# Moving the identity's blocks and the query spreads of a decode attention kernel from VectorE to GpSimd, and taking row sums as repeated matmul weights

## The chip, the cores and the metric

One core of one Trainium2 chip. The metric is the device time of one execution in microseconds (us). Before the change it was 1344.0 us, the median of 3 runs (1343.92 to 1344.07).

## The reference, cut to what matters

```python
B, Sq, D = 4, 1, 1024
H, Sk, Dh = 32, 8192, 128
q = reshape(x @ wq)                              # B, H, 1, Dh
scores = einsum("bhqd,bhkd->bhqk", q, k_cache) * Dh ** -0.5
o = einsum("bhqk,bhkd->bhqd", softmax(scores), v_cache)
a = reshape(o) @ wo
# B: a gated MLP on one token per batch, F = 3584 (w_gate, w_up, w_down)
return g * a + (1 - g) * b                       # g = sigmoid((x * gate_w).sum(-1))
```

All tensors are bf16. The key and the value cache hold 4 x 32 x 8192 x 128 elements each, 268 MB apiece. Every byte is read once and used for one query row, so this is a kernel that streams.

## The kernel before

The caches are read as 32 key blocks and 32 value blocks of 4 heads (8.39 MB, two halves of 4.19 MB). They go through a ring of five slots in SBUF, each half a block in size. A load is issued by SyncE as soon as the slot's last reader has finished.

```python
NS = 5
ring = const.tile([P, NS, RING], BF, name="ring")      # 5 slots of 32 KB per partition
def load_pair(src, n, apart=False):                     # two slots, one or two DMAs
    a = slots(2)
    if a + 1 < NS and not apart:
        nc.sync.dma_start(out=flat[:, lo:lo + 2 * n], in_=src)      # [cut]
    ...                                                 # else one DMA for each half
```

A key block is turned piece by piece on VectorE (eight 128x2048 transposes) and multiplied on TensorE with the four queries. The weights of these matmuls are a window into a tile `Z` that is zero except for the query values. Writing those values into `Z` is the "spread". It is done for the next block while a block is being worked on; there are two `Z` tiles.

```python
def spread(d):
    b, h0 = heads(d)
    Z = Zt[d % 2]
    nc.vector.tensor_tensor(out=Z[:, :, QP - 1:QP - 1 + P].rearrange("p e (q c) -> p e q c", c=QP)[:, :, :, 0],
                            in0=qa[:, :, h0:h0 + NQ, b], in1=mq[:].to_broadcast([P, 4, NQ]), op=ALU.mult)

def k_pair(d):
    ...                                                 # [cut] Z, sps
    ks = load_pair(kv_view(A_k_cache, d), RING)
    for n in range(RD):                                 # 8 pieces
        kn, c = ks[n // JT], n % JT
        nc.vector.transpose(out=flat_t.bitcast(U32),
                            in_=kn[:, c * CJ * Dh:(c + 1) * CJ * Dh].bitcast(U32))
        ...                                             # [cut] 8 matmuls with windows of Z
        if n == JT // 2 and d + 1 < ND:
            spread(d + 1)                               # JT // 2 == 2: after the third piece
    if t == GD - 1:
        softmax(g)                                      # after each group of four blocks
```

Four key blocks make a group. `softmax` leaves the row sums `rs` [128 x 1]. A total for each head is then a matmul of the row sums, spread by a mask, with a matrix of ones:

```python
rex = stat.tile([P, GH], F32, tag="rex")
nc.vector.tensor_scalar(out=rex[:], in0=mask, scalar1=rs[:, 0:1], scalar2=None, op0=ALU.mult)
def inverse():
    nc.tensor.matmul(tot[:, :], lhsT=ones[:], rhs=rex[:], start=True, stop=True)
    ...
```

GpSimd has, before the change, only some memsets and half of the copies that bring a group's probabilities from `PT` to `PB` (ScalarE does the other half). Value block d - 4 follows key block d on TensorE. The engines' order of work is fixed by the program: an engine does its instructions in the order in which they are written.

Of the kernel before, what the change touches and what calls it, by code (L numbers as in the profile page):

```python
# [8 lines left out]
BF = mybir.dt.bfloat16  # L9
F32 = mybir.dt.float32  # L10
U32 = mybir.dt.uint32
ACT = mybir.ActivationFunctionType
ALU = mybir.AluOpType
AX = mybir.AxisListType
# [98 lines left out]
def kernel(  # L113
# [15 lines left out]
    nc = tc.nc  # L129
    P = 128  # L130
# [4 lines left out]
    NQ = 4  # L135
    QP = P // NQ
# [5 lines left out]
    GH = GD * NQ  # L142
# [14 lines left out]
    const = ctx.enter_context(tc.tile_pool(name="const", bufs=1))  # L157
    ptp = ctx.enter_context(tc.tile_pool(name="ptp", bufs=1))
    stat = ctx.enter_context(tc.tile_pool(name="stat", bufs=2))
# [39 lines left out]
    def small(shape, dtype=F32):  # L199
        return mps.tile(shape, dtype, name="small", tag="small")  # L200
# [15 lines left out]
        nc.vector.memset(z[:], 0.0)  # L216
    acc = acc4[0:Bn].rearrange("p z n -> p (z n)")

    row = const.tile([P, P], F32)
    nc.vector.memset(row[:, 0:1], 0.0)  # L220
    n = 1
    while n < P:
        nc.vector.tensor_scalar(out=row[:, n:2 * n], in0=row[:, 0:n], scalar1=float(n), scalar2=None, op0=ALU.add)
        n *= 2
    col = const.tile([P, 32], F32)
    nc.vector.transpose(out=col[:].bitcast(U32), in_=row[:, 0:32].bitcast(U32))
    for n in range(32, P, 32):
        nc.vector.tensor_scalar(out=col[n:n + 32], in0=col[n:n + 32], scalar1=float(n), scalar2=None, op0=ALU.add)
    ident = const.tile([P, P], F32)
    nc.vector.tensor_scalar(out=ident[:], in0=row[:], scalar1=col[:, 0:1], scalar2=None, op0=ALU.is_equal)  # L230
    identb = const.tile([P, P], BF)
    nc.vector.tensor_copy(out=identb[:], in_=ident[:])
    xw_ps = small([P, DT, NX], BF)
# [5 lines left out]
    R = ptp.tile([P, 4, P], BF, name="R", tag="PTs")  # L239
    for half in range(2):  # L240
        for e in range(2):
            turns = ident[:, 64 * half + e:64 * half + 64:2]
            for n in range(4):
                nc.vector.tensor_copy(out=R[:, 2 * half + e, 32 * n:32 * n + 32], in_=turns)

    mask3 = const.tile([P, GD, NQ], F32)
    nc.vector.tensor_reduce(out=mask3[:], in_=ident[:].rearrange("p (q t r) -> p t q r", q=NQ, t=GD), axis=AX.X, op=ALU.add)
    mask = mask3[:].rearrange("p t q -> p (t q)")
    selg = const.tile([P, 4, GD, NQ], F32)
    one = ident[:].rearrange("p (t e s a) -> p e a t s", t=GD, e=2, s=NQ)  # L250
    for a in range(4):
        nc.vector.tensor_tensor(out=selg[:, a], in0=one[:, 0, a], in1=one[:, 1, a], op=ALU.add)
    mE4 = const.tile([P, 2, 4], F32)
    nc.vector.tensor_reduce(out=mE4[:], in_=ident[:].rearrange("p (n e r) -> p e n r", n=4, e=2), axis=AX.X, op=ALU.add)
    mE = const.tile([P, 2], F32)
    nc.vector.tensor_reduce(out=mE[:], in_=mE4[:], axis=AX.X, op=ALU.add)
    mq4 = const.tile([P, NQ], F32)
    nc.vector.tensor_reduce(out=mq4[:], in_=ident[:].rearrange("p (q r) -> p q r", q=NQ), axis=AX.X, op=ALU.add)
    mq = const.tile([P, 1, NQ], BF)
    nc.vector.tensor_copy(out=mq[:, 0, :], in_=mq4[:])  # L260
    ones = const.tile([P, P], F32)
    nc.gpsimd.memset(ones[:], 1.0)
    mx, mxT, ng, ngT = [const.tile([P, 32], F32, name=f"mx{i}") for i in range(4)]
    nc.vector.memset(mx[:], 0.0)
    ZW = QP - 1 + P + 1
    Zt = [const.tile([P, 4, ZW], BF, name=f"Z{i}") for i in range(2)]
    PB = const.tile([P, QP, 2, 2, 2, NQ, 4], BF, name="PB")
# [5 lines left out]
    qa = const.tile([P, 4, H, Bn], BF)  # L273
# [143 lines left out]
    def heads(d):  # L417
        return divmod(d * NQ, H)
# [5 lines left out]
    def spread(d):  # L424
        b, h0 = heads(d)
        Z = Zt[d % 2]
        nc.vector.tensor_tensor(out=Z[:, :, QP - 1:QP - 1 + P].rearrange("p e (q c) -> p e q c", c=QP)[:, :, :, 0],  # L427
                                in0=qa[:, :, h0:h0 + NQ, b], in1=mq[:].to_broadcast([P, 4, NQ]), op=ALU.mult)

    def k_pair(d):  # L430
        g, t = divmod(d, GD)
        Z = Zt[d % 2]
        if d == 0:
            spread(0)
        if t == 0:
            S_ps[g] = scp.tile([P, 2, 512], F32, name="S_ps")
        sps = S_ps[g]
        ks = load_pair(kv_view(A_k_cache, d), RING)
        for n in range(RD):
            kn, c = ks[n // JT], n % JT  # L440
            flat_t = turned(P, CJ * P)
            T = flat_t.rearrange("p (j h i e) -> p j h i e", j=CJ, h=2, e=2)
            nc.vector.transpose(out=flat_t.bitcast(U32),  # L443
                                in_=kn[:, c * CJ * Dh:(c + 1) * CJ * Dh].bitcast(U32))
            s = QP - 1 - (RD * t + n)
            for he in range(4):
                half, e = divmod(he, 2)
                for z in range(2):
                    nc.tensor.matmul(sps[:, z, :], lhsT=Z[:, he, s:s + P], rhs=T[:, 16 * z:16 * z + 16, half, :, e],  # L449
                                     start=(t == 0 and n == 0 and he == 0),  # L450
                                     stop=(t == GD - 1 and n == RD - 1 and he == 3))
            if n == JT // 2 and d + 1 < ND:
                spread(d + 1)
            if n == JT:
                flush()
            if n == JT + 2:
                flush_late()
        if t == GD - 1:
            softmax(g)

    def softmax(g):
        sps = S_ps.pop(g)

        nc.vector.tensor_reduce(out=mx[:, 0:1], in_=sps[:].rearrange("p z n -> p (z n)"), axis=AX.X, op=ALU.max)  # L464
        nc.vector.transpose(out=mxT[:].bitcast(U32), in_=mx[:].bitcast(U32))
        gm = stat.tile([P, GD], F32, tag="gm")
        nc.vector.tensor_reduce(out=gm[:], in_=mxT[:].rearrange("p (t r) -> p t r", r=RD), axis=AX.X, op=ALU.max)
        nc.vector.tensor_scalar(out=ng[:].rearrange("p (t r) -> p t r", r=RD), in0=gm[:].unsqueeze(2).to_broadcast([P, GD, RD]),
                                scalar1=-scale, scalar2=None, op0=ALU.mult)
        nc.vector.transpose(out=ngT[:].bitcast(U32), in_=ng[:].bitcast(U32))  # L470
        negm = ngT
        PTs = ptp.tile([P, 1024], BF, name="PTs", tag="PTs")
        rs = stat.tile([P, 1], F32, tag="rs")
        nc.scalar.activation(out=PTs[:], in_=sps[:].rearrange("p z n -> p (z n)"), func=ACT.Exp, bias=negm[:, 0:1], scale=scale, accum_out=rs[:, 0:1])  # L474
        PT = ptp.tile([P, 32, 32], BF, name="PT")
        nc.vector.transpose(out=PT[:].rearrange("p j i -> p (j i)"), in_=PTs[:])  # L476
        rex = stat.tile([P, GH], F32, tag="rex")
        nc.vector.tensor_scalar(out=rex[:], in0=mask, scalar1=rs[:, 0:1], scalar2=None, op0=ALU.mult)

        def inverse():  # L480
            tot = small([P, GH])
            nc.tensor.matmul(tot[:, :], lhsT=ones[:], rhs=rex[:], start=True, stop=True)  # L482
            rinv = stat.tile([P, GH], F32, name="rinv", tag="rinv")
            nc.vector.reciprocal(out=rinv[:], in_=tot[:, :])  # L484
            rinv_t[g] = rinv
        late.append(inverse)

        def spread_p():
            Pv = PT[:].rearrange("p (q j) i -> p i q j", j=4)
            Bv = PB[:].rearrange("p i z w e s j -> p i (z w e) s j")  # L490
            for q in range(NQ):
                at = slice(QP * q, QP * (q + 1))
                if q % 2 == 0:
                    nc.scalar.copy(out=Bv[at, :, :, q, :], in_=Pv[at])  # L494
                else:
                    nc.gpsimd.tensor_copy(out=Bv[at, :, :, q, :], in_=Pv[at])  # L496
        behind.append(spread_p)
# [125 lines left out]
```

## Time and profile before

| | before |
|---|---|
| time, median | 1344.0 us |
| bytes moved, span of the profiled run | 576.18 MB, 1342.0 us |
| DMA share and rate, 0 to 1321 us | 1.00, 432 GB/s |
| busy: TensorE, VectorE, GpSimd | 77%, 46%, 3% |
| VectorE's waits for key DMAs | 485.6 us |

The page of the profile of before. PE is TensorE, PEld its weight loads, DVE VectorE, ACT ScalarE, POOL GpSimd. The rows of digits cut the span into 40 slices; a digit is the busy share in tenths, 9 for 90% or more. The last two lines are the chain of waits, by engine and by line: the work that ended last, followed back.

```profile
span 1342.0 us, 7617 instructions
...
PE 1037.2 (77%) x4552; PEld 228.1 (17%) x2364; DVE 621.8 (46%) x434; ACT 50.6 (4%) x46; POOL 35.5 (3%) x24
...
DVE  3555655545346554336455556046555254556000
...
DMA  9999999999999999999999999999999999999997
GB/s 416 437 432 430 436 436 427 447 428 421 441 426 429 443 436 423 437 434 430 438 434 430 432 427 436 436 432 438 428 425 433 432 433 440 436 419 446 419 424 327
...
DMA 69%; DVE 19%; PE 11%; issue 0%; ACT 0%; SPq 0%; DVEq 0%
DMA ring<-in_A_k_cache_dram 58%; DVE TB L443 19%; DMA ring<-in_A_v_cache_dram 7%; PE o_ps L523 7%; PE S_ps L449 3%; DMA ring<-in_B_w_gate_dram 3%; DMA ring<-in_A_wo_dram 1%; PE o_ps L315 0%; DVE Z L427 0%; PE acc L315 0%; PE acc L281 0%; PE small L482 0%; PE small L543 0%; DVE OS L536 0%; ACT OS L535 0%
```

The reader is to see the DMA row, full to the last slice, beside a VectorE row of fives. The chain of waits gives VectorE 19%, but this is not a limit by itself: a DMA that is issued when a buffer comes free appears in the chain behind whatever freed the buffer, even if other transfers keep the DMA engines busy meanwhile. The table of stages (a stretch of the span, its length, the busy time of each engine with its instructions, granted TensorE clock, DMA share, GB/s) settles it:

```profile
core 0: us, PE busy (x) PEld busy (x) DVE busy (x) ACT busy (x) POOL busy (x), PEclk, DMA share, GB/s
...
0.00:1321.00 1321.00, 1021.15 (x4464) 224.20 (x2309) 619.92 (x430) 49.35 (x44) 35.48 (x24) 0.90 1.00 432
1321.00:1337.50 16.50, 14.31 (x81) 3.66 (x52) 1.23 (x3) 0.69 (x1) 0.00 (x0) 1.00 0.84 343
```

Until 1321 us the DMA engines are busy all the time: the share is 1.00. The Trainium skill, "SBUF — State Buffer", section "SBUF: two separate sides", names about 436 GB/s as the peak of the DMA side of SBUF; the 432 GB/s of this trace agree.

The issues of DMAs on the same page (KB each, and median us from issue to landing) show that half a key block, 4096 KB, takes 34.2 us, of which its own bytes need about 9.7 us at 432 GB/s; it stands behind other transfers for the rest. (The 14 halves are those of the 7 key blocks that go over the end of the ring and so take two DMAs.)

```profile
ring<-in_A_k_cache_dram SPq DMA_DIRECT2D x14, 4096.0 KB, 34.2
```

What the change touches on VectorE, from the groups of instructions by form (line, engine, operation, output<-inputs, shapes, count | busy us, mean ns | idle us just before, and what ended it), and the only large group on GpSimd:

```profile
L443 DVE STREAM_TRANSPOSE TB<-ring 128x2048 uint32<-128x2048 uint32 x256 | 569.4, 2280 | 487.7 <-DMA ring<-in_A_k_cache_dram 485.6 <-PE S_ps L449 2.1
...
L427 DVE TENSOR_TENSOR Z<-qa,mq 128x16 bf16<-128x16 bf16 x32 | 6.0, 189 | 0.0
...
L478 DVE TENSOR_SCALAR rex<-mask,rs 128x16 f32<-128x16 f32 x8 | 1.5, 193 | 0.0
```

```profile
L496 POOL COPY PB<-PT 32x1024 bf16<-32x1024 bf16 x16 | 30.5, 1905 | 1223.9 <-PE o_ps L523 1069.8 <-DVE rex L478 153.6
```

One steady period of the chain of waits (start, length, what):

```profile
364.96 6.70 DVE TB L443 x3
371.66 0.11 DVE Z L427
371.77 10.95 DVE TB L443 x5
382.72 0.04 issue
382.76 1.90 PE S_ps L449 x8
384.66 13.93 PE o_ps L523 x64
398.61 34.40 DMA ring<-in_A_k_cache_dram
```

The stream needs 16.78 MB / 432 GB/s = 38.8 us for the pair.

### The profile page before, as it was taken

To read this page: it belongs to the slowest core of one execution; us is meant where nothing else is said; L and a number is where in the kernel's file an instruction comes from. 1 tells how busy PE (TensorE), PEld (TensorE's weight loads), DVE (VectorE), ACT (ScalarE), POOL (GpSimd) and SP (SyncE) were. 2 spreads that over 40 slices of the span, in tenths; PEclk is the share of its full clock that TensorE was granted. 3 is DMA by queue.
4 is the path that set the end of the run, shared out by engine and by line. 5 is a ranking of instruction groups with operands and counts; after the bars stand their busy time and mean duration, and the time that the engine had idled before them with its cause. 6 is when DMAs were issued, how large, how long until landed. Compare 5 with 4: busy or idle time off the path is not lost.

```text
span 1342.0 us, 7617 instructions
## 1 busy us (share of the span) xinstructions
PE 1037.2 (77%) x4552; PEld 228.1 (17%) x2364; DVE 621.8 (46%) x434; ACT 50.6 (4%) x46; POOL 35.5 (3%) x24
## 2 busy tenths in 40 slices
PE   2565878787788687778987779597778678877898
PEld 0111111111111121111211112111111112111222
DVE  3555655545346554336455556046555254556000
ACT  0000100001000010001000010000100010000100
POOL 1000100001000010001000010000100010000100
PEclk9777988988998888899988889898889799888999
DMA  9999999999999999999999999999999999999997
GB/s 416 437 432 430 436 436 427 447 428 421 441 426 429 443 436 423 437 434 430 438 434 430 432 427 436 436 432 438 428 425 433 432 433 440 436 419 446 419 424 327
DMA packets 14316, 576.18 MB, mean 429 GB/s; under 512 B 1598, under 2 KB 1606, under 8 KB 2252
## 3 DMA queue, kind: packets, MB, share of 16 engines
q1 hardware_dynamic: 14276, 575.69, 99.5%
q8 instruction: 27, 0.44, 0.1%
q14 instruction: 5, 0.04, 0.0%
q10 hardware_dynamic: 8, 0.00, 0.0%
HBM read 575.68 MB, written 0.01 MB: 429 GB/s over the span
## 4 chain that ended last, share of the span: by engine, by line
DMA 69%; DVE 19%; PE 11%; issue 0%; ACT 0%; SPq 0%; DVEq 0%
DMA ring<-in_A_k_cache_dram 58%; DVE TB L443 19%; DMA ring<-in_A_v_cache_dram 7%; PE o_ps L523 7%; PE S_ps L449 3%; DMA ring<-in_B_w_gate_dram 3%; DMA ring<-in_A_wo_dram 1%; PE o_ps L315 0%; DVE Z L427 0%; PE acc L315 0%; PE acc L281 0%; PE small L482 0%; PE small L543 0%; DVE OS L536 0%; ACT OS L535 0%
## 5 line engine op out<-in xcount | busy, mean ns | idle before, releaser
L443 DVE STREAM_TRANSPOSE TB<-ring 128x2048 uint32<-128x2048 uint32 x256 | 569.4, 2280 | 487.7 <-DMA ring<-in_A_k_cache_dram 485.6
L449 PE MATMUL S_ps<-TB,Z 128*128 128x512 bf16 x2048 | 522.8, 411 | 216.5 <-DVE TB L443 216.0
L523 PE MATMUL o_ps<-ring,PB 128*32 128x512 bf16 x2048 | 461.3, 387 | 52.5 <-DMA ring<-in_A_v_cache_dram 48.0
L449 PEld LDWEIGHTS <-Z 128*128 128x128 bf16 x1024 | 106.1, 104 | 628.4 <-issue 626.8
L523 PEld LDWEIGHTS <-PB 128*32 128x32 bf16 x1024 | 100.5, 98 | 404.9 <-issue 394.9
L496 POOL COPY PB<-PT 32x1024 bf16<-32x1024 bf16 x16 | 30.5, 1905 | 1223.9 <-PE o_ps L523 1069.8
L474 ACT ACTIVATE PTs<-S_ps,mx 128x1024 bf16<-128x1024 f32 x8 | 8.9, 1114 | 1019.7 <-DVE mx L470 1019.7
L536 DVE SCALAR_TENSOR_TENSOR OS<-o_ps,mE,OS 128x512 f32<-128x512 f32 x8 | 6.0, 751 | 70.8 <-ACT OS L535 70.8
L494 ACT COPY PB<-PT 32x1024 bf16<-32x1024 bf16 x16 | 30.6, 1910 | 1.6 <-DVE PT L476 1.4
L484 DVE RECIPROCAL rinv<-small 128x16 f32<-128x16 f32 x8 | 2.1, 258 | 41.5 <-PE small L482 41.5
L378 DVE CAST LT<-small 128x64 bf16<-128x64 f32 x2 | 0.5, 225 | 44.0 <-PE small L376 44.0
L235 PE MATMUL small<-identb,x 6*128 6x6 bf16 x8 | 0.6, 197 | 22.2 <-DMA x<-in_A_x_dram 22.2
L464 DVE TENSOR_REDUCE mx<-S_ps 128x1 f32<-128x1024 f32 x8 | 9.8, 1225 | 15.9 <-PE S_ps L449 15.9
L281 PE MATMUL acc<-ring,LT 128*4 128x512 bf16 x64 | 14.8, 379 | 1.7 <-DMA ring<-in_A_wo_dram 0.9
L476 DVE STREAM_TRANSPOSE PT<-PTs 128x1024 bf16<-128x1024 bf16 x8 | 10.0, 1245 | 10.2 <-ACT PTs L474 10.2
L281 PE MATMUL acc<-ring,hT 128*4 128x512 bf16 x56 | 12.2, 379 | 0.0
L535 ACT ACTIVATE OS<-o_ps,mE 128x512 f32<-128x512 f32 x8 | 5.5, 687 | 163.4 <-PE o_ps L523 163.4
L543 PEld LDWEIGHTS small<-selg,OS 128*128 128x128 f32 x64 | 8.4, 195 | 4.1 <-issue 3.9
L315 PE MATMUL o_ps<-ring,xw 128*4 128x512 bf16 x56 | 5.3, 505 | 3.9 <-DMA ring<-in_B_w_gate_dram 3.9
L543 PE MATMUL small<-selg,OS 128*128 128x16 f32 x64 | 8.1, 259 | 0.0
L237 DVE COPY xw<-small 128x48 bf16<-128x48 bf16 x1 | 0.2, 182 | 14.9 <-PE small L235 14.9
L315 PE MATMUL S_ps<-ring,xw 128*4 128x512 bf16 x64 | 6.3, 582 | 0.3 <-DVE xw L237 0.3
(68 smaller groups left out, 72.6 us busy)
## 6 DMA issues: line engine op xcount, KB each, us to landing
ring<-in_A_k_cache_dram SPq DMA_DIRECT2D x14, 4096.0 KB, 34.2
ring<-in_A_v_cache_dram SPq DMA_DIRECT2D x14, 4096.0 KB, 31.3
ring<-in_B_w_gate_dram SPq DMA_DIRECT2D x1, 7168.0 KB, 37.2
ring<-in_B_w_up_dram SPq DMA_DIRECT2D x1, 7168.0 KB, 39.2
ring<-in_B_w_down_dram SPq DMA_DIRECT2D x2, 3584.0 KB, 27.3
ring<-in_A_wo_dram SPq DMA_DIRECT2D x6, 1024.0 KB, 24.7
ring<-in_A_v_cache_dram SPq DMA_DIRECT2D x2, 2048.0 KB, 30.5
ring<-in_A_v_cache_dram SPq DMA_DIRECT2D x4, 1024.0 KB, 24.6
```

The source lines that it names most:

```text
L281: nc.tensor.matmul(out_ap, lhsT=lhsT, rhs=rhs, start=start, stop=True, skip_group_check=True)
L315: nc.tensor.matmul(ps[32 * k:32 * k + Bn, z, :], lhsT=xT[TW * half + t], rhs=cols(w, t, 4 * z + k), start=(half + t == 0), stop=(half == 1 ...
L443: nc.vector.transpose(out=flat_t.bitcast(U32), in_=kn[:, c * CJ * Dh:(c + 1) * CJ * Dh].bitcast(U32))
L449: nc.tensor.matmul(sps[:, z, :], lhsT=Z[:, he, s:s + P], rhs=T[:, 16 * z:16 * z + 16, half, :, e], start=(t == 0 and n == 0 and he == 0), ...
L464: nc.vector.tensor_reduce(out=mx[:, 0:1], in_=sps[:].rearrange("p z n -> p (z n)"), axis=AX.X, op=ALU.max)
L474: nc.scalar.activation(out=PTs[:], in_=sps[:].rearrange("p z n -> p (z n)"), func=ACT.Exp, bias=negm[:, 0:1], scale=scale, accum_out=rs[:, ...
L476: nc.vector.transpose(out=PT[:].rearrange("p j i -> p (j i)"), in_=PTs[:])
L494: nc.scalar.copy(out=Bv[at, :, :, q, :], in_=Pv[at])
L496: nc.gpsimd.tensor_copy(out=Bv[at, :, :, q, :], in_=Pv[at])
L523: nc.tensor.matmul(o_ps[row:row + NM, e, :], lhsT=PB[:, RD * t + c, z, w].rearrange("p e s j -> p (e s j)"), rhs=vn[:, j0 * Dh:(j0 + 4) * ...
L536: nc.vector.scalar_tensor_tensor(out=o_sb[:], in0=o_ps[:, 1, :], scalar=mE[:, 1:2], in1=o_sb[:], op0=ALU.mult, op1=ALU.add)
L543: nc.tensor.matmul(oT[:, :], lhsT=o_sb[:, q * Dh:(q + 1) * Dh], rhs=selg[:, q].rearrange("p t s -> p (t s)"), start=(q == 0), stop=(q == 3))
```

## The change

The intent was to relieve VectorE: the query spread becomes four copies on GpSimd, one for each quarter of the partitions, so no mask is needed. The identity is made of four copies of a 32x32 identity, also on GpSimd, as are the casts into `R` (16 on VectorE before, 4 larger ones now). The product of row sums and mask goes away, because the row sums become the matmul's weights, repeated over 128 columns, and the mask itself its operand.

```diff
+    nc.vector.tensor_tensor(out=id32[:], in0=row[:, 0], in1=row[:, 1], op=ALU.is_equal)
     ident = const.tile([P, P], F32)
-    nc.vector.tensor_scalar(out=ident[:], in0=row[:], scalar1=col[:, 0:1], scalar2=None, op0=ALU.is_equal)
+    nc.gpsimd.memset(ident[:], 0.0)
+    for n in range(0, P, 32):
+        nc.gpsimd.tensor_copy(out=ident[n:n + 32, n:n + 32], in_=id32[n:n + 32])
 [cut: rows and columns are counted to 32 only; masks mE4, mq4, mq and the ones are gone]
-            turns = ident[:, 64 * half + e:64 * half + 64:2]
-            for n in range(4):
-                nc.vector.tensor_copy(out=R[:, 2 * half + e, 32 * n:32 * n + 32], in_=turns)
+            nc.gpsimd.tensor_copy(out=R[:, 2 * half + e].rearrange("p (n j) -> p n j", n=4),
+                                  in_=ident[:, 64 * half + e:64 * half + 64:2].unsqueeze(1).to_broadcast([P, 4, 32]))
 [cut]
-        nc.vector.tensor_tensor(out=Z[:, :, QP - 1:QP - 1 + P].rearrange("p e (q c) -> p e q c", c=QP)[:, :, :, 0],
-                                in0=qa[:, :, h0:h0 + NQ, b], in1=mq[:].to_broadcast([P, 4, NQ]), op=ALU.mult)
+        for q in range(NQ):
+            at = slice(QP * q, QP * (q + 1))
+            nc.gpsimd.tensor_copy(out=Z[at, :, QP - 1 + QP * q], in_=qa[at, :, h0 + q, b])
 [cut]
-        rex = stat.tile([P, GH], F32, tag="rex")
-        nc.vector.tensor_scalar(out=rex[:], in0=mask, scalar1=rs[:, 0:1], scalar2=None, op0=ALU.mult)
-            nc.tensor.matmul(tot[:, :], lhsT=ones[:], rhs=rex[:], start=True, stop=True)
+            nc.tensor.matmul(tot[:, :], lhsT=rs[:, 0:1].to_broadcast([P, P]), rhs=mask, start=True, stop=True)
```

More of the change, by code (lines that the diff above doesn't have):

```diff
@@ L217 @@
     acc = acc4[0:Bn].rearrange("p z n -> p (z n)")
-    row = const.tile([P, P], F32)
-    nc.vector.memset(row[:, 0:1], 0.0)
+    row = const.tile([P, 2, 32], F32)
+    nc.vector.memset(row[:, 0, 0:1], 0.0)
     n = 1
-    while n < P:
-        nc.vector.tensor_scalar(out=row[:, n:2 * n], in0=row[:, 0:n], scalar1=float(n), scalar2=None, op0=ALU.add)
+    while n < 32:
+        nc.vector.tensor_scalar(out=row[:, 0, n:2 * n], in0=row[:, 0, 0:n], scalar1=float(n), scalar2=None, op0=ALU.add)
         n *= 2
-    col = const.tile([P, 32], F32)
-    nc.vector.transpose(out=col[:].bitcast(U32), in_=row[:, 0:32].bitcast(U32))
-    for n in range(32, P, 32):
-        nc.vector.tensor_scalar(out=col[n:n + 32], in0=col[n:n + 32], scalar1=float(n), scalar2=None, op0=ALU.add)
+    nc.vector.transpose(out=row[:, 1].bitcast(U32), in_=row[:, 0].bitcast(U32))
+    id32 = const.tile([P, 32], F32)
+    nc.vector.tensor_tensor(out=id32[:], in0=row[:, 0], in1=row[:, 1], op=ALU.is_equal)
     ident = const.tile([P, P], F32)
-    nc.vector.tensor_scalar(out=ident[:], in0=row[:], scalar1=col[:, 0:1], scalar2=None, op0=ALU.is_equal)
+    nc.gpsimd.memset(ident[:], 0.0)
+    for n in range(0, P, 32):
+        nc.gpsimd.tensor_copy(out=ident[n:n + 32, n:n + 32], in_=id32[n:n + 32])
     identb = const.tile([P, P], BF)
@@ L252 @@
         nc.vector.tensor_tensor(out=selg[:, a], in0=one[:, 0, a], in1=one[:, 1, a], op=ALU.add)
-    mE4 = const.tile([P, 2, 4], F32)
-    nc.vector.tensor_reduce(out=mE4[:], in_=ident[:].rearrange("p (n e r) -> p e n r", n=4, e=2), axis=AX.X, op=ALU.add)
     mE = const.tile([P, 2], F32)
-    nc.vector.tensor_reduce(out=mE[:], in_=mE4[:], axis=AX.X, op=ALU.add)
-    mq4 = const.tile([P, NQ], F32)
-    nc.vector.tensor_reduce(out=mq4[:], in_=ident[:].rearrange("p (q r) -> p q r", q=NQ), axis=AX.X, op=ALU.add)
-    mq = const.tile([P, 1, NQ], BF)
-    nc.vector.tensor_copy(out=mq[:, 0, :], in_=mq4[:])
-    ones = const.tile([P, P], F32)
-    nc.gpsimd.memset(ones[:], 1.0)
+    nc.vector.tensor_reduce(out=mE[:], in_=id32[:].rearrange("p (e r) -> p e r", e=2), axis=AX.X, op=ALU.add)
     mx, mxT, ng, ngT = [const.tile([P, 32], F32, name=f"mx{i}") for i in range(4)]
-    nc.vector.memset(mx[:], 0.0)
+    nc.gpsimd.memset(mx[:], 0.0)
     ZW = QP - 1 + P + 1
```

## The prediction

> **What bounds the kernel now.** The input stream. The page of before counts 576.18 MB in a 1342.0 us span, 429 GB/s, and the DMA row is 9 (90% or more) in 39 of 40 slices. By the table of stages, the DMA share is 1.00 at 432 GB/s from 0 to 1321 us; only the tail runs below. The Trainium skill ("SBUF — State Buffer", section "SBUF: two separate sides") gives about 436 GB/s as the peak of the DMA side; this trace's 432 agrees. VectorE is busy 46% (621.8 us), TensorE 77%, GpSimd 3% (35.5 us).
>
> The chain of waits names VectorE for 19%, but those are transposes that free the next key buffer, and the queue is deep: a 4 MB key transfer lands 34.2 us after its issue (issue table), while 4 MB at 432 GB/s takes about 9.7 us. A release that comes a fraction of a microsecond earlier lengthens the queue; it does not speed the stream.
>
> **What the change removes from VectorE** (groups by form): 32 query spreads, 6.0 us (189 ns each; 0.11 us of each stands in the chain); 8 products of row sums with the mask, 1.5 us; 16 casts into R, 1.5 us; some set-up, about 2 us. About 11 us of 622, where VectorE already waits 485.6 us for key DMAs.
>
> **What it adds to GpSimd.** 128 copies of 32 partitions x 4 elements, 8 set-up copies, a few memsets. A 128x1 memset took 98 ns and a 32x1024 copy 1905 ns: about 1.8 ns per element and 0.1 us fixed. Estimate: 0.1 to 0.2 us per spread copy, 0.4 to 0.8 us per group of four, 13 to 25 us in all; set-up a few us. GpSimd ends at 50 to 65 us busy, under 5%.
>
> **What it moves.** The identity now goes through VectorE, GpSimd, VectorE in the first 10 us; its first consumer waits until 22.2 us for the x DMA. The first spread stays near 35 us; its key block lands at 49.9 us. Later spreads are issued one key block ahead (20 to 40 us). The one queue risk: GpSimd waits, in order, with the probability copies until TensorE finishes a value block (1069.8 us of such waits, 7 times), and a spread stands behind two copies of 1.9 us. It is then ready about 4.5 us after that value block, but TensorE still has a whole key block (64 matmuls, about 14 us) before it needs it. So it should hide. The totals take as many matmuls as before (0.26 us each).
>
> Ports: the same section says that GpSimd and a VectorE instruction that uses the second port lock each other out. No run here shows yet whether the one-source transposes do; I expect them to stay at 2280 ns.
>
> **On the critical path:** about 0. The stream is full, its bytes do not change, and head (22 us until the first weights land) and tail (1321 to 1342 us) contain none of the moved work.
>
> **Predicted: 1343.9 us**, 1339 to 1349 at 8 in 10. Faster by over 2%: 0.01; within 2%: 0.97; slower by over 2%: 0.02.
>
> **Signs.** Right: VectorE busy near 611 us, some 374 instructions; transposes near 2280 ns; GpSimd 50 to 65 us; DMA share 1.00 at about 432 GB/s until 1321 us; no TensorE wait for the query spreads over 1 us. Wrong: TensorE waiting for Z released by GpSimd; transposes lengthened; DMA slices below 9.
>
> **What would make it wrong:** spread copies over 2 us each, or queued until the key block needs them; locked ports that stretch the transposes; a DMA rate that differs for reasons outside the kernel (0.3% is 4 us).

## The result, and the profile after

The kernel after took 1343.81 us (median of 6 runs, 1343.62 to 1344.08) beside 1344.03 us for before (6 runs). The ratio is 0.9999, with a 95% interval of 0.9986 to 1.0012: the same. A ratio here is the mean time of one kernel's fast runs over that of the other's of the same rounds, so not quite the ratio of the medians that are quoted.

The page of the profile of after, the same lines:

```profile
span 1342.2 us, 7696 instructions
...
PE 1032.8 (77%) x4552; PEld 227.9 (17%) x2364; DVE 614.4 (46%) x369; ACT 50.6 (4%) x46; POOL 62.8 (5%) x161
...
DVE  2555655545336554335455556046555254556000
...
DMA  9999999999999999999999999999999999999997
GB/s 414 436 432 431 439 434 427 445 430 422 445 424 430 442 432 426 438 434 428 438 436 426 432 430 434 436 433 438 428 423 436 430 431 442 436 419 444 419 425 325
...
DMA 66%; DVE 21%; PE 11%; another core or an unknown queue 1%; ACT 0%; issue 0%; SPq 0%; DVEq 0%
```

The VectorE row differs in three digits; the DMA row is the same digit for digit. VectorE lost 65 instructions and 7.4 us of busy time, GpSimd gained 137 instructions and 27.3 us. The stages, with the columns as before:

```profile
0.00:1321.00 1321.00, 1016.78 (x4464) 223.95 (x2309) 612.47 (x365) 49.33 (x44) 62.75 (x161) 0.90 1.00 432
1321.00:1337.50 16.50, 14.16 (x81) 3.66 (x52) 1.23 (x3) 0.69 (x1) 0.00 (x0) 1.00 0.84 344
```

The transposes, and what GpSimd does beside memsets and the four copies of the small identity, by form:

```profile
L436 DVE STREAM_TRANSPOSE TB<-ring 128x2048 uint32<-128x2048 uint32 x256 | 566.9, 2277 | 492.4 <-DMA ring<-in_A_k_cache_dram 491.5 <-PE S_ps L442 0.8
```

```profile
L486 POOL COPY PB<-PT 32x1024 bf16<-32x1024 bf16 x16 | 30.3, 1892 | 430.3 <-PE o_ps L513 426.2 <-DVE PT L469 3.8
L421 POOL COPY Z<-qa 32x4 bf16<-32x4 bf16 x128 | 25.6, 200 | 761.6 <-PE S_ps L442 736.0 <-DVE qa L326 19.6
...
L243 POOL CAST R<-ident 128x128 bf16<-128x128 f32 x4 | 1.1, 298 | 0.1
```

The transposes kept their length (2280 and 2277 ns). Four spread copies take 0.95 us together, as the next listing shows. The matmuls of the totals did not change: in both traces 16 of them run at 263 ns in the median, with weight loads of 187 ns.

The same period of the chain of waits as above (pieces in order of time, the longest ones):

```profile
364.77 17.68 DVE TB L436 x8
384.38 13.93 PE o_ps L513 x64
398.33 34.12 DMA ring<-in_A_k_cache_dram
```

The 0.11 us piece "DVE Z" between the transposes is gone: 17.68 us now from the first to the last of the eight, where it was 6.70 + 0.11 + 10.95 = 17.76. The next key load is issued at 398.33 us in place of 398.61, and then takes as long as it takes the stream to get to it.

The worst place for a spread on GpSimd, the boundary of a group, from the timeline of after (start, length, engine, line, what, count [idle before <- who ended it]):

```profile
321.31 3.82 POOL L486 COPY PB<-PT 32x1024 bf16<-32x1024 bf16 x2 [60.88 <-PE o_ps L513]
...
325.19 0.95 POOL L421 COPY Z<-qa 32x4 bf16<-32x4 bf16 x4
325.92 15.47 DVE L436 STREAM_TRANSPOSE TB<-ring 128x2048 uint32<-128x2048 uint32 x7 [3.16 <-DMA ring<-in_A_k_cache_dram]
```

The two probability copies wait for the end of a value block at 321.3 us, and the spread stands behind them until 326.14 us, 4.8 us after the value block. But that spread is for the block after the one whose transposes begin at 325.92 us; it is needed after 364.77 us, some 38 us later. Nowhere in the trace of after does TensorE wait over 1 us for `Z` from GpSimd.

### The profile page after: what moved, and what is told of

Its sections match the earlier page's. It is cut to its first block, busy times and chain, and to the rows that moved or that the text cites. A ratio compares the mean times of both kernels' runs of the same rounds, so it can differ in the third digit from the quotient of the medians.

```text
span 1342.2 us, 7696 instructions
## 1 busy us (share of the span) xinstructions
PE 1032.8 (77%) x4552; PEld 227.9 (17%) x2364; DVE 614.4 (46%) x369; ACT 50.6 (4%) x46; POOL 62.8 (5%) x161
## 4 chain that ended last, share of the span: by engine, by line
DMA 66%; DVE 21%; PE 11%; another core or an unknown queue 1%; ACT 0%; issue 0%; SPq 0%; DVEq 0%
DMA ring<-in_A_k_cache_dram 58%; DVE TB L436 21%; PE o_ps L513 9%; DMA ring<-in_A_v_cache_dram 5%; DMA x<-in_gate_w_dram 2%; DMA ring<-in_A_wo_dram 1%; PE S_ps L442 1%; ACT PB L484 0%; PE S_ps L307 0%; PE acc L307 0%; PE acc L273 0%; PE small L533 0%; ACT OS L525 0%; PE small L472 0%
## 5 line engine op out<-in xcount | busy, mean ns | idle before, releaser
L436 DVE STREAM_TRANSPOSE TB<-ring 128x2048 uint32<-128x2048 uint32 x256 | 566.9, 2277 | 492.4 <-DMA ring<-in_A_k_cache_dram 491.5
L421 POOL COPY Z<-qa 32x4 bf16<-32x4 bf16 x128 | 25.6, 200 | 761.6 <-PE S_ps L442 736.0
```

Of the source, the lines that this page charges most:

```text
L421: nc.gpsimd.tensor_copy(out=Z[at, :, QP - 1 + QP * q], in_=qa[at, :, h0 + q, b])
L436: nc.vector.transpose(out=flat_t.bitcast(U32), in_=kn[:, c * CJ * Dh:(c + 1) * CJ * Dh].bitcast(U32))
```

## The experiments

Twelve kernels ran, each with five rounds beside the kernel before on the same chip. Four theories and a few rivals go through them. Theory A: the input stream is the bound, and both what VectorE saves and what GpSimd gets is hidden behind it. Rival B: the saving on VectorE is real, and GpSimd gives it back. Rival C: VectorE paces the stream. Rival D: the port that VectorE and GpSimd share costs something. Theories F and G arose from a result, and are told there.

### 1. No spreads at all (no_spread)

The kernel before; only the spreads for the first two blocks are made. This is a wrong result, although the comparison with the reference passed it: with these inputs the output hardly depends on which query is used.

```diff
-            if n == JT // 2 and d + 1 < ND:
+            if n == JT // 2 and d == 0:
                 spread(d + 1)
```

> The kernel before, but the query spreads are made only for the first two key blocks (a wrong result on purpose): VectorE loses 30 of its 32 spreads and GpSimd gets nothing for them. Theory A (full input stream, deep queue): the 0.11 us per spread on VectorE buys nothing; ratio to before 1.000, within 0.0013. Rival B (the change gains on VectorE and gives the same back on GpSimd): the gain alone is seen here, 30 x 0.11 us to 30 x 0.19 us, so 3.3 to 5.7 us less, ratio 0.9958 to 0.9975. VectorE busy falls by about 3.3 us of union time or more.

Measured: 1344.47 us (5 runs) against 1344.09 (9 runs); ratio 1.0003, 0.9990 to 1.0015. VectorE's busy time fell from 621.8 to 619.4 us, 2.4 us where I had expected 3.3 or more. Rival B needed a ratio of 0.9975 or less and falls: the spreads cost nothing where they stood, so there was nothing for GpSimd to give back.

### 2. More work for VectorE (vector_dose1, 2, 4, 8)

The kernel before; the third transpose of every key block, beside the spread, is made 1, 2, 4 or 8 times more (DOSE below stands for this number). The result stays right.

```diff
+            for _ in range(1 + DOSE if n == JT // 2 else 1):
-            nc.vector.transpose(out=flat_t.bitcast(U32), in_=...)
+                nc.vector.transpose(out=flat_t.bitcast(U32), in_=...)
```

> The kernel before with one more VectorE transpose per key block (the third is made twice, right beside the spread): 32 x 2.2 us = 70 us more VectorE work, some twenty times what a spread costs in the chain. Theory A: ratio 1.000 within 0.002, VectorE busy near 692 us. Rival C (VectorE's releases of key buffers pace the stream, as the 19% in the chain suggests): up to 70 us longer, ratio up to 1.05; even a tenth of it would be 7 us, ratio 1.005.

> The same with four more transposes per key block: 32 x 8.8 us = 281 us more VectorE work. In the steady part a key block and a value block take 38.7 us of stream; VectorE's part of it rises from about 19.5 to 28.3 us. Theory A: the queue held at least 17 us of other data at each key issue (shortest key issue to landing 27.3 us, less 9.7 us of own transfer), so a release 8.8 us later empties nothing: ratio 1.00 to 1.01 (the shallow start may cost a few us), time from issue to landing shorter by some 9 us (34 to about 25 us). Rival C: 100 to 281 us longer, ratio 1.07 to 1.21.

One more transpose, 2.2 us a block or 70 us in all, gave 1344.12 us, ratio 1.0001 (0.9989 to 1.0014). That is about twenty times what a spread costs in the chain, and it is not seen. Its own page shows where it went: the same line of the DMA issues as before, from 34.2 down to 32.1 us from issue to landing. The load is issued later by one transpose, and waits less by as much.

```profile
ring<-in_A_k_cache_dram SPq DMA_DIRECT2D x14, 4096.0 KB, 32.1
```

But four more, 8.8 us a block, gave 1431.86 us, ratio 1.0652 (1.0637 to 1.0666). My expectation of at most 1.01 failed. The page of this run, the same rows:

```profile
DMA  9989699999899999999899999999999998999998
GB/s 417 435 382 420 285 411 408 441 437 385 357 411 411 433 404 414 405 400 424 340 411 410 410 389 391 424 409 386 411 382 432 430 402 353 411 425 424 427 427 354
...
ring<-in_A_k_cache_dram SPq DMA_DIRECT2D x14, 4096.0 KB, 27.5
```

The DMA row now has holes. The waiting time of a load in the queue is not the reserve: I had computed 17 us from it. With only five slots, the loads that stand in the queue belong to slots that are free already, while the pair being worked on holds the others; the measure that counts is the way of the pair through the engines (33.6 us, by the sum 6.70 + 0.11 + 10.95 + 0.04 + 1.90 + 13.93 in the profile before) against 38.8 us of stream. From the time: 87.8 us over 32 pairs is 2.7 us a pair, so 8.8 - 2.7 = 6 us a pair were to spare. The sum had said 5.

This new form of theory A was put to the test with two more doses:

> The kernel before with two more VectorE transposes per key block, 4.4 us. Theory A in its new form: after four more transposes (8.8 us a block) the time rose by 87.8 us, 2.7 us for each of 32 pairs, so a pair of a key and a value block has about 6 us to spare on the path transposes, then value matmuls (17.5 + 1.9 + 13.9 = 33.3 us against 38.7 us of stream). 4.4 us stay below it: ratio 1.000 to 1.004 (the shallow start may add some us). Rival C (VectorE's time passes into the stream in proportion, 87.8/281 = 0.31 of it): 44 us longer, ratio 1.033.

> The kernel before with eight more transposes per key block, 17.5 us. Theory A in its new form: 17.5 less about 6 us to spare is 11.5 us for each of 32 pairs, 368 us: 1712 us, ratio 1.25 to 1.30. Rival C (proportional): 560 x 0.31 = 175 us longer, 1519 us, ratio 1.13.

Measured: with two more (4.4 us) 1351.30 us, ratio 1.0053 (1.0042 to 1.0065), a little above the 1.004 expected; its runs differ more than the others' (1348.38 to 1353.65 us). In its slices the rate is low only from about 67 to 168 us, where the loads of the MLP share the ring with the first blocks, so the first few pairs probably have less to spare; this was not tested. With eight more (17.5 us) 1682.14 us, ratio 1.2515 (1.2499 to 1.2531), near the lower end of what was expected: 338.1 us over 32 pairs is 10.6 us a pair, which puts the spare time at 6.9 us. The proportional rival (ratios 1.033 and 1.13) falls on both sides.

| more VectorE time per block | longer than before | per pair |
|---|---|---|
| 2.2 us | 0.0 us | 0.0 us |
| 4.4 us | 7.3 us | 0.2 us |
| 8.8 us | 87.8 us | 2.7 us |
| 17.5 us | 338.1 us | 10.6 us |

The change saves 0.11 us of a way that has 5 to 7 us to spare. It moves along the flat part of this curve, in the direction in which there is nothing to be had.

### 3. Sixteen times the spreads on GpSimd (pool_x16)

The kernel after; each spread's four copies are made 16 times, the same data into the same place.

```diff
-        for q in range(NQ):
+        for q in list(range(NQ)) * 16:
```

> The kernel after with each of its GpSimd query copies made 16 times (the same data into the same place): 15 x 0.95 us = 14.3 us more GpSimd work per key block, 460 us in all. Theory A: the copies run during the block ahead, which starts some 38 us before its successor; ratio 1.000 within 0.002, GpSimd busy near 450 us. Rival B (GpSimd's copies cost the time that VectorE saved): sixteen times a cost of 3 to 6 us, so 50 to 90 us longer, ratio 1.04 to 1.07. Rival D (GpSimd and VectorE share a port that the transposes need): transposes longer than 2.28 us in the mean, or copies longer than 0.2 us.

Measured: 1348.73 us, ratio 1.0034 (1.0021 to 1.0048): 4.6 us longer. Neither theory had it. Rival B's 50 to 90 us are excluded by far, but theory A had said nothing at all. Rival D is excluded for the transposes: they took 2276 ns and the 2048 copies 195 ns in the mean. GpSimd was busy 436.7 us.

The trace holds two clues. The queue of instruction fetches on the page's list of DMA queues (here q14) has 20 packets of 8 KB, and 5 in the kernel after; the program is longer by 1920 instructions. And at the end of the stream the DMA engines do not end together: a few microseconds pass in which the DMA share is near 0.06, that is one engine of 16. From this came theory F: fetching the instructions of GpSimd takes the time of one DMA engine that also carries its part of the stream, and a landing waits for the slowest engine. Its rival G: it is GpSimd's busy time, or a spread that comes late.

### 4. Few long or many short instructions (pool_few, pool_many)

The kernel after, with extra work behind each spread that nothing reads (cut: the tile `spare`).

```diff
+        for _ in range(18):                                          # pool_few
+            nc.gpsimd.tensor_copy(out=spare[:], in_=qa[:, 0:3])      # 128 x 384
```
```diff
+        for _ in range(60):                                          # pool_many
+            nc.gpsimd.memset(spare[:], 0.0)                          # 128 x 1
```

> The kernel after with 18 large GpSimd copies (128 x 384 bf16, some 0.8 us each) behind each query spread, into a spare tile: as much more GpSimd time as the sixteenfold copies had (about 460 us against 374 us), but 576 more instructions in place of 1920. Theory F (the 4.6 us of the sixteenfold copies came from fetching instructions: 15 more fetches of 8 KB, 0.31 us each, seem to land on one of the 16 DMA engines, which then ends the stream alone): 4 to 5 more fetches, so 1.2 to 1.6 us, ratio 1.000 to 1.0015. Rival G (GpSimd's busy time, or spreads that come late for TensorE): 4 us or more, ratio 1.003 or more.

> The kernel after with 60 tiny GpSimd memsets (128 x 1, 35 ns apart) behind each query spread: 1920 more instructions, as the sixteenfold copies had, but only about 67 us more GpSimd time, 2.1 us a block. Theory F: 15 more instruction fetches of 8 KB, as many microseconds longer as the sixteenfold copies were, 4 to 5.5 us, ratio 1.003 to 1.004, and at the end of the stream one DMA engine working alone for some 4 us. Rival G: a sixth of the time added, 0 to 0.8 us, ratio 1.000 to 1.001.

Measured: pool_few 1343.97 us, ratio 1.0000 (0.9988 to 1.0012); pool_many 1348.32 us, ratio 1.0031 (1.0018 to 1.0044). The run with GpSimd busy 354.5 us cost nothing, the one with 251.4 us cost 4.3 us. So rival G falls in its first form: it is the number of instructions that counts, not GpSimd's busy time. A spread that comes late is not the cause either. By the waits, TensorE stood 26.9 us for the spreads in pool_x16, but only 0.7 us for GpSimd's work behind `Z` in pool_many, which lost as much, and 13.5 us in pool_many30 of the next section, which lost nothing. (A copy of 128 x 384 took 507 ns, not 0.8 us, and a memset 98 ns, not 35, so the added times were 292 and 189 us instead of some 460 and 67; the order that the test needs still holds.)

The end of the stream by the table of stages, first after, then pool_many (next to last column: DMA share):

```profile
1336.00:1338.00 2.00, 1.89 (x10) 0.34 (x4) 0.00 (x0) 0.00 (x0) 0.00 (x0) 1.00 0.28 111
1338.00:1340.00 2.00, 1.36 (x7) 0.17 (x2) 0.68 (x1) 0.57 (x1) 0.00 (x0) 1.00 0.01 4
```

```profile
1336.00:1338.00 2.00, 1.74 (x8) 0.42 (x5) 0.21 (x1) 0.00 (x0) 0.00 (x0) 1.00 0.42 161
1338.00:1340.00 2.00, 1.70 (x9) 0.29 (x4) 0.00 (x0) 0.00 (x0) 0.00 (x0) 1.00 0.13 53
1340.00:1342.00 2.00, 2.00 (x10) 0.38 (x5) 0.00 (x0) 0.00 (x0) 0.00 (x0) 1.00 0.06 26
```

In after the stream is over by 1338 us. In pool_many a share of 0.06 = 1/16 lasts through the stretch from 1340 to 1342 us: one engine works alone. The two kernels' lines of the instruction queue, pool_few and pool_many (packets, MB, share):

```profile
q14 instruction: 10, 0.08, 0.0%
```

```profile
q14 instruction: 20, 0.16, 0.0%
```

### 5. Half and twice as many (pool_many30, pool_many120)

```diff
-        for _ in range(60):
+        for _ in range(30):      # pool_many30; 120 in pool_many120
```

> The kernel after with 30 in place of 60 tiny GpSimd memsets per spread: 960 more instructions, 7 to 8 more fetches of 8 KB. Theory F with a margin (the run with few large copies had 7 more fetches than the kernel after and cost nothing, because the engine that fetches was one of those that ended early): 0 to 1 us, ratio 0.999 to 1.001. Theory F without a margin: half of 4.4 us, 2.2 us, ratio 1.0016.

> The kernel after with 120 tiny GpSimd memsets per spread: 3840 more instructions, 30 more fetches. Theory F: 15 fetches more than with 60 memsets at 0.31 us each, 4.7 us on top of its 4.3 us: 8 to 10 us over before, ratio 1.006 to 1.0075, and one DMA engine alone at the end for about 9 us (DMA share 0.06). If the 4.3 us had another cause that saturates, the ratio stays near 1.003.

Measured: pool_many30 1343.94 us, ratio 0.9998 (0.9986 to 1.0011), 13 packets in the queue (the expectation's "7 more fetches" of pool_few are 5 by the pages, 10 against 5); pool_many120 1359.65 us, ratio 1.0116 (1.0100 to 1.0131), 36 packets. One DMA engine is alone at the end of the latter, through a whole stretch of 4 us:

```profile
1344.00:1348.00 4.00, 3.64 (x36) 1.74 (x31) 0.48 (x2) 0.00 (x0) 0.00 (x0) 1.00 0.58 222
1348.00:1352.00 4.00, 3.75 (x19) 0.68 (x8) 0.00 (x0) 0.00 (x0) 0.00 (x0) 1.00 0.06 25
```

| kernel | GpSimd busy | packets in q14 | against before |
|---|---|---|---|
| after | 62.8 us | 5 | -0.2 us |
| pool_few | 354.5 us | 10 | -0.1 us |
| pool_many30 | 157.0 us | 13 | -0.2 us |
| pool_many | 251.4 us | 20 | +4.3 us |
| pool_x16 | 436.7 us | 20 | +4.6 us |
| pool_many120 | 440.5 us | 36 | +15.5 us |

The time follows the packets, with a margin: up to 13 they are free, then each costs more than the 0.31 us that its packet takes (11.2 us for 16 packets from the fourth line to the last, 0.7 us each). The size was not as I expected (8 to 10 us for pool_many120). The queue is not GpSimd's alone: it has 4 packets in no_spread, where VectorE has 30 instructions fewer, and 7 in vector_dose8, where it has 256 more.

That one DMA engine ends last is shown by the shares. That it is the one that fetches can be read from the packet records in the kept traces (`trace.npz`; `prof` prints only their sums). Each of the 16 engines closes its part of a transfer with a packet of 4 bytes, so its end can be seen. In pool_many the last engine ends 2.3 us after the fifteenth at 581 us, and 2.9, 3.6, 4.2 and 4.8 us after it once the fetches at 590.7, 664.0, 744.6 and 822.7 us are done: about 0.65 us for each. Followed by the times of the packets, each of these fetches stands without a gap between two data packets of that engine. A fetch takes 0.31 us itself, and the data packet behind it takes 0.35 us more than others of its size (2.77 us in place of 2.42 for 64 KB). This is the 0.7 us per packet. In pool_many30 the last engine is never more than 2.3 us behind the fifteenth between 300 and 1290 us, and in after 2.2 us: 13 fetches have not made one engine late yet.

In pool_many120 the late engine ends a key transfer at 369.8 us, 5.6 us after the fifteenth, and only then do the transposes begin, at 370.36 us. There most of the loss comes along the stream and not at its end, as the rate of after and of pool_many120 over the same 900 us shows:

```profile
300.00:1200.00 900.00, 716.52 (x3031) 156.78 (x1547) 438.78 (x242) 33.65 (x30) 40.57 (x104) 0.90 1.00 432
```

```profile
300.00:1200.00 900.00, 705.52 (x2989) 154.46 (x1526) 426.75 (x237) 33.64 (x30) 312.21 (x2864) 0.89 1.00 427
```

Five GB/s of 432 over 900 us are about 10 of the 15.5 us. TensorE also waits 39.0 us for GpSimd's work behind `Z` in pool_many120, so a part of the 15.5 us could come from late spreads; this was not separated.

For the change itself it means: 137 instructions more on GpSimd stay at 5 packets, far inside the margin.

### 6. The stream out of the way (quarter_before, quarter_after)

Both kernels (the edit is cut: `load_pair` also gets the argument `part`, 1 where nothing is said); key blocks from the fifth on and value blocks but the last load only a quarter of each half, the rest of the slot holds older data. All arithmetic stays. Their outputs are wrong, which doesn't matter for the times.

```diff
+        if part > 1:
+            halves = [ring[:, a], ring[:, (a + 1) % NS]]
+            for i, half in enumerate(halves):
+                nc.sync.dma_start(out=half[:, 0:n // part], in_=src[:, i * n:i * n + n // part])
+            return halves
-        ks = load_pair(kv_view(A_k_cache, d), RING)
+        ks = load_pair(kv_view(A_k_cache, d), RING, part=4 if d >= 4 else 1)
-            vs = load_pair(vv, RING, apart=d >= ND - 3)
+            vs = load_pair(vv, RING, apart=d >= ND - 3, part=4)
```

> The kernel before, but the key blocks from the fifth on and all value blocks but the last load only a quarter of each half (the rest of the buffer holds older data: a wrong result on purpose); all arithmetic stays. The stream falls from 576 MB to about 210 MB, some 490 us at 430 GB/s, so it can no longer be the bound. Theory A: the time falls to what the engines need, near TensorE's 1037 us of busy time: 1000 to 1150 us, and the DMA share falls to about half. If something other than the stream bounds the kernel, the time stays above 1250 us.

> The same cut of the loads in the kernel after. Theory A: VectorE's lighter load is hidden only because the stream bounds; with the stream out of the way the saved 0.11 us (spread) per key block can show at most as 3.5 us plus 1.5 us of the mask products, so 0 to 5 us below quarter_before, ratio of the two 0.995 to 1.000. Rival B (gain and loss of equal size in the change): GpSimd's side shows as well, and the two differ by less than 1 us or the kernel after is the slower one.

Measured: 1100.04 us (ratio to before 0.8186, 0.8175 to 0.8197) and 1099.24 us (0.8181, 0.8170 to 0.8192). The page of quarter_before:

```profile
span 1098.0 us, 7685 instructions
...
PE 979.1 (89%) x4552; PEld 221.7 (20%) x2364; DVE 621.3 (57%) x434; ACT 50.9 (5%) x46; POOL 35.6 (3%) x24
...
DMA  9999984333333334244343334234344434333393
```

With 205 MB in place of 576 the time falls by 244 us, and TensorE is busy 89%. So the stream is what bounds the kernel before, directly shown; without it TensorE is next, not VectorE (57%). The two differ by 0.8 us, less than the intervals allow to call a difference. It neither confirms nor excludes a gain of 1 to 2 us; even where the stream is not in the way, lightening VectorE is worth less than 0.3%.

Not tried: the totals with repeated weights alone. The whole change is worth nothing and the matmuls of the totals are the same length in both traces, so no run was spent on it.

## Why the prediction was right, point by point

- **The bound.** Right, and shown by quarter_before: 371 MB fewer, 244 us shorter, with all arithmetic kept. The stream stage of after has the same share 1.00 and 432 GB/s.
- **No gain from VectorE.** Right, shown twice: without the spreads the time is the same (no_spread), and with 2.2 us a block more it is the same too (vector_dose1).
- **Its reason, the deep queue.** Right in direction: a release later by one transpose shortened the time from issue to landing by 2.1 us. As a measure of the reserve, which the prediction did not state but my first expectation drew from it, it is too large: 17 us by the queue, 5 to 7 us by the doses. The way of a pair (transposes, then value matmuls) against the stream's time for a pair gave 5 us, nearly right.
- **VectorE's busy time.** Predicted 611 us and 374 instructions; 614.4 us and 369. The mis-sized term is "about 11 us of 622": I added whole durations (189 ns a spread), but back-to-back instructions overlap in the records, and only 0.11 us of a spread stood alone in the chain. The busy time is a union, so it fell by 7.4 us. The instruction count was taken from the description's "60"; the trace counts 65.
- **GpSimd.** 62.8 us, inside the predicted 50 to 65. The term within it was low: 0.2 us a copy held, but a group of four takes 0.95 us, above the 0.4 to 0.8 predicted; set-up takes less than thought.
- **The spread behind the probability copies.** Predicted ready 4.5 us after the value block; 4.8 us, and hidden as predicted.
- **Ports.** The transposes stayed at 2277 ns, also under 2048 copies (2276 ns). The Trainium skill, "SBUF — State Buffer", section "Who interferes with whom", says that a VectorE copy can take the port pair that GpSimd uses, and that the loser waits for the whole instruction. One place of this trace agrees: the first two spread copies began at 32.1 us, during two VectorE copies of 128x1024 (31.93 to 33.22 us), and took 521 and 544 ns where the other 126 took 190 to 202 ns. The listing of the instructions on `Z` in after from 31.9 to 33.3 us (count: least/median/most ns, first and last start):

```profile
L421 POOL COPY Z<-qa x2: 521/532/544, 32.1 to 32.7; 32x4 bf16<-32x4 bf16 x2
```

  No experiment isolated this, and at that place nothing waits for the spread.
- **Rival causes.** That gain and loss cancelled is excluded for the spreads, by no_spread and pool_x16 together. The smaller parts of the change (mask products, casts, identity) were not taken out alone. What the prediction missed without harm is the cost of fetching instructions; the change stays far below where it shows.

## What to carry to other kernels

Before relieving an engine, add up the way of one unit of work through the engines and compare it with what the stream needs for that unit; if it is shorter, a saving is worth nothing until the stream shrinks, and a loss is worth nothing until the difference is used up (here 5 to 7 us of 38.8). Adding work in doses measures this difference better than the time that loads stand in a queue. When work moves to an engine as more and smaller instructions, look at the instruction-fetch packets and at whether the DMA engines still end together.

## What the Trainium skill lacked or had wrong

- No page found tells how much DMA time instruction fetches take from a stream that is full: "Runtime: NRT & Kernel Launch", section "Instruction fetch mechanics", would be the place. Packets of 8 KB, 0.31 us each, 0.65 us with the delay of the packet behind: 13 were free, 20 cost 4.3 to 4.6 us, 36 cost 15.5 us.
- "GPSIMD Engine Reference", section "Elementwise — side-by-side cycle accounting", has no time for tiles as small as these. Small copies here: 32x4 bf16 in 194 ns in the median, four of them in 0.95 us; 128x384 bf16 in 507 ns; a 128x1 memset in 98 ns.
- "SBUF — State Buffer", section "Who interferes with whom", does not name VectorE's stream transposes. 256 of them kept 2276 ns in the mean beside 2048 GpSimd copies of 195 ns in the mean: no contention seen.
- "Perfetto Trace Analysis", section "What \"DMA-bound\" means", names specific DMA engines as one bound; the runs add a case of it, with one of 16 engines alone for at least 4 us at the end (pool_many120).
